# Attention of state tokens followed by two feed-forward nets: the opening's order, the third batch's route and the half chunk's place in the second sweep

## The chip, the cores and the metric

The kernel runs on one core of a Trainium2 chip. The metric is the device time of one launch in microseconds (us), the median over repeated runs. TensorE is called PE in the profile, its weight loads PEld, VectorE is DVE, ScalarE is ACT, GpSimd is POOL, and SP is the engine that issues nearly all DMAs. All matrix work is in 32-bit floats; most of it is done in three passes over a high and a low part (HIxHI, LOxHI, HIxLO), each part in the type fp32r.

## The reference, cut to what matters

```python
# x (8, 8, 512, 64): 8 batches, 8 heads, 512 tokens; state (8, 8, 32, 64): 32 state tokens
scores = scale * x @ state^T ; a = softmax(scores, over the 32 state tokens)
xread = a @ state                                   # (512 tokens)
scores2 = scale * state @ x^T ; a2 = softmax(scores2, over the 512 tokens)
sread = a2 @ x                                      # (32 state tokens)
x = concat([xread, sread], axis=tokens)             # 544 tokens a batch, 4352 in all
x = relu(x @ w_in)**2 @ w_out                       # 512 -> 2048 -> 512
a = x @ w1 ; b = x @ w2 ; out = ((a * b) @ w3) @ w_out2   # 512 -> 1024 -> 1024 -> 512
```

The weights come as 64-bit floats and are turned into 32-bit ones on the chip.

## The kernel before, in words

**Tokens.** The 512 tokens of batch b are chunk c = b (c = 0..7). The 8 x 32 state tokens make a ninth chunk, c = B = 8, of 256 columns: half a chunk.

**First stage (up to about 690 us).** The loop `order` runs over tiles (c, f): 16 tiles f of 128 hidden units for each chunk. The chunks 0 and 1 are interleaved (c0 f0-3, c1 f0-3, c0 f4-7, c1 f4-7, c0 f8-15, c1 f8-15), and then each chunk follows alone; "tile 20" below is the twentieth of this order, counted from 0. For each tile PE makes h (`h_tile`, L442: 6 matmuls), ACT and DVE make relu, square and the split (`act_h`), and two tiles later PE adds into four y banks (`y_tile`, L480: 12 matmuls). Between the tiles stand side jobs: `side[i]` behind h of tile i and `late[i]` behind the y part. They hold the conversions of weights from 64 bits (`conv`, five DVE instructions and one ACT instruction, and for w_out a split), `make_sw` (state times w_in, L413, 16 matmuls, needed by four h tiles), and the attention of the batch that comes next (`att_slots`).

**Attention of a batch** (`att_steps`): transposed x (`xpose` or `turn_x`), `scores` (L290), the softmax over x tokens (`soft2`, then `a2_T`, `sread`, `sread_T`) and that over state tokens (`soft1a`, `soft1b`, `a_T`). Batches below `BLK` = 3 take the PE route: x comes as rows (`load_x`), ACT copies it (`make_x`), PE transposes it with 16 matmuls against the identity (L277) and ACT copies the result; `soft1a` and `a_T` transpose on PE, too (L321, L345). Batches from `BLK` on take the block route: x is loaded twice, once as blocks of 32 columns (`load_xb`, eight DMAs of 64 KB for four heads) that DVE transposes block by block (`turn_x`, L257), once as rows (`load_xn`); `soft1a` and `a_T` transpose on DVE (L316, L341).

**The opening** (L513 to L542) loads the state of the first four chunks on ACT's queue (`load_st(0)`), x of batch 0, four half blocks of w_in, w_out's first block, x of batch 1 and the other half of the state; then batch 0's attention up to `at[1]`, whose last DVE instruction is `first`; the DVE work of `side[0]` is queued behind it.

**What sets the order.** A planner puts the instructions of each engine into one fixed order, from the program's order and its own estimate of when each is ready; `tc.issue_after(ins)` queues those instructions of a block that run on the same engine as `ins` behind it. Each engine then works in order. PSUM has eight banks: two "m" (side jobs), two "h", and "y0" to "y3". A tile tag with n buffers makes its n+1st user wait. The loads of weights, of `load_x` and of `load_xb` share the tag "raw" with three buffers. DMAs use eight semaphores in turn, so that a ninth waits until the first has landed; the queue behind it on the same engine waits with it.

**Second stage.** w3 times w_out2 is made first (`w34_rows`), so that the second net is a product (a*b) and one matmul. Its hidden units are done in two sweeps of half each (s = 0, 1). In each sweep pairs of chunks go through `quad` (L795, seven products) and `out_tile` (L876); `ab9` (L850) and `out_tile(B, ...)` do the same for the half chunk. `out_tile` of sweep 0 stores partial sums (`o_scr`), that of sweep 1 loads them (`load_o`), adds and writes the output, in one DMA of 256 KB for a chunk's tile and four of 64 KB for the half chunk's. Sweep 0 begins with the half chunk, sweep 1 ends with it. Between the sweeps `make_w` splits the weights of the second half and two DMAs load the second half of w34 (L950) into the buffers that sweep 0's last `out_tile` reads.

Of the kernel before, what the change touches and what calls it, by code (L numbers as in the profile page):

```python
# [8 lines left out]
F32 = mybir.dt.float32  # L9
# [11 lines left out]
def kernel(  # L21
# [24 lines left out]
    P = 128  # L46
# [9 lines left out]
    HI, LO = 0, 1  # L56
    BLK = 3

# [12 lines left out]
    def bank_m(name):  # L71
        return psum.tile([P, 512], F32, tag="m", bufs=2, name=name)
# [194 lines left out]
    def att_steps(b):  # L267
# [69 lines left out]
        def a_T(r):  # L337
            e = v["e1", r].rearrange("p k n -> p (k n)")
            if b >= BLK:
                ps = v["S", r]  # L340
                nc.vector.transpose(out=ps, in_=e)  # L341
            else:
                ps = bank_m("ps_a")
                for j in range(J):
                    nc.tensor.transpose(ps[:, j * P:(j + 1) * P], e[:, j * P:(j + 1) * P], ident)  # L345
            t = pa.tile([P, 2, 512], F32R, tag=f"aT{r}", bufs=2, name=f"aT{r}")
            aT_t[b, r] = t
            return split(t[:, HI], t[:, LO], ps)
# [40 lines left out]
    def att_slots(b):  # L389
        if b >= B:  # L390
            return [[] for _ in range(NF)]
        xp, sc, s2, s1a, s1b, at, a2t, sr, srt = att_steps(b)
        if b >= BLK:
            return [
                [sc], [], [s2[0], s1a[0]], [],
                [s1b[0], s2[1]], [a2t[0]], [at[0], s1a[1]], [sr[0]],
                [s1b[1], srt[0]], [a2t[1]], [at[1]], [sr[1]], [srt[1]], [], [], [],
            ]
        return [
            [xp[0]], [xp[1]], [xp[2]], [xp[3]],  # L400
            [sc], [s2[0]], [a2t[0]], [s1a[0], s2[1]],
            [sr[0], s1b[0]], [srt[0]], [a2t[1], at[0]], [sr[1], s1a[1]],
            [srt[1], s1b[1]], [at[1]], [], [],
        ]

    SW = {}

    def make_sw(b, fg, cols=slice(0, 512)):
        pss = [bank_m("ps_sw") for _ in range(G)]
        for k in range(HG):  # L410
# [84 lines left out]
    def load_st(half):  # L495
# [3 lines left out]
        for k in range(HG):  # L499
            for r in range(G):  # L500
                (nc.sync if half else nc.scalar).dma_start(
                    t[k * NS:(k + 1) * NS, :, r, :],
                    state[half * (B // 2):(half + 1) * (B // 2), 2 * k + r].rearrange("b n d -> n b d"),
                )
        st.append(t.rearrange("p b r d -> p b (r d)"))

    def make_st(half):
# [3 lines left out]
        nc.scalar.copy(stT[:, 4 * half:4 * half + 4].rearrange("p b k n -> p (b k n)"), ps)  # L511

    load_st(0)  # L513
    load_x(0, 0, True)
    load_x(0, 1, True)
    load_win0(0, 0, True)
    make_x(0, 0, nc.vector)
    make_x(0, 1, nc.scalar)
    load_win0(0, 1, True)
    load_win0(1, 0, True)  # L520
    load_win0(1, 1, True)
# [3 lines left out]
    load_st(1)  # L525
    for g in range(G):
        make_x(1, g, nc.scalar, True)
    make_st(0)
    xp, sc, s2, s1a, s1b, at, a2t, sr, srt = att_steps(0)
    xp1, sc1, s21, s1a1, s1b1, at1, a2t1, sr1, srt1 = att_steps(1)  # L530
    for step in xp:
        step()
    sc()
    make_win0(0, 0)
# [5 lines left out]
    s1b[1]()  # L540
    make_sw(0, 0, slice(0, 256))
    first = at[1]()  # L542

    convs = [("win", 1, k) for k in range(ND)] + [("wo", f) for f in range(4, 8)]
# [30 lines left out]
    late = {}  # L575
    side[0] = [lambda: make_win0(1, 0), s2[0], lambda: make_win0(1, 1), xp1[0], xp1[1], a2t[0]]
    side[1] = [lambda: make_sw(0, 0, slice(256, 512)), lambda: make_wout(0), xp1[2], xp1[3], sr[0], s2[1], sc1]
    side[2] = [conv, s1a1[0], srt[0], a2t[1], s1b1[0], sr[1], at1[0]]
    side[3] = [conv, s21[0], srt[1], s1a1[1], a2t1[0], conv, s1b1[1], sw(1, 0), at1[1]]
    side[4] = [conv, s21[1], sr1[0], lambda: make_st(1)]  # L580
# [9 lines left out]
    for b in range(2, B):  # L590
# [5 lines left out]
        for g in range(G):  # L596
            i = 9 + g if b == 2 else (b - 2) * NF + 12 + g
            if b < BLK:
# [318 lines left out]
    make_pair(raw)  # L917
    for m in range(QM):
        ab9(m)
    for t in range(n_out(B)):  # L920
        out_tile(B, t, 0)
    for s, todo in enumerate((pairs, pairs[::-1])):
        for i, (c0, c1) in enumerate(todo):
            for m in range(QM):
# [3 lines left out]
                if m == 1 and i + 1 == len(todo) and s == 0:  # L928
                    raw = load_w(1)
            if i + 1 == len(todo) and s == 1:  # L930
                raw = load9()
            outs = [(c, t) for c in (c0, c1) for t in range(n_out(c))]
# [3 lines left out]
            for n, (c, t) in enumerate(outs):  # L936
# [3 lines left out]
                with tc.issue_after(last.ins):  # L940
                    if n == 0 and i + 1 < len(todo):
                        make_pair(raw)
                    if n == 0 and i + 1 == len(todo) and s == 0:
                        make_w(raw)
                if n == 3 and i + 1 == len(todo) and s == 1:
                    make9(raw)
            if s == 0 and i + 1 == len(todo):
                for j in range(N1 // 4):
                    w34_t[N1 // 4 + j] = wpool.tile([P, 2, 2, DM], F32R, tag="wi0", bufs=2, name="w34b")
                    nc.sync.dma_start(f32(w34_t[N1 // 4 + j]), w34_s[j])  # L950
    for t in range(n_out(B)):
        load_o(B, t)
    for m in range(QM):
        ab9(m)
    for t in range(n_out(B)):
        out_tile(B, t, 1)

# [28 lines left out]
```

## Time and profile before

| | us |
|---|---|
| time, median of 3 runs (lowest, highest) | 1285.98 (1285.95, 1286.9) |
| the profiled execution's own time | 1288.85 |
| its span | 1287.0 |
| PE busy in the span | 1253.1 (97%) |
| DVE busy | 798.0 (62%) |
| ACT busy | 655.1 (51%) |

The profiled execution is 2.87 us above the median of the runs. "Busy" counts an engine's instructions from start to end as the profile has them; PE's ends are modelled, so that what one matmul costs is read from the distance between starts.

### The profile page before, as it was taken

Reading aid. Unit: us, or ns where it says so; the run is one execution under the profiler, and the core shown is the slowest. Engines: PE = TensorE matmul, PEld = TensorE weight load, DVE = VectorE, ACT = ScalarE, POOL = GpSimd, SP = SyncE. Lnnn points to the kernel's source line nnn. Section 1 sums busy time; section 2 is a strip of 40 time slices with the busy share of each in tenths; the row PEclk is TensorE's granted clock in tenths of the full one; section 3 lists DMA queues with packets and bytes.
Section 4 is the critical chain, followed back from the end, with each engine's and each line's share of the span. In section 5 each row is a group of like instructions: output and inputs, shape, how many; then the busy total and the mean of one; then the engine's idle time right before and its main releaser. Section 6 shows DMA issues by size and latency. Waiting matters only on the chain.

```text
span 1287.0 us, 16895 instructions
## 1 busy us (share of the span) xinstructions
PE 1253.1 (97%) x6392; PEld 986.7 (77%) x6392; DVE 798.0 (62%) x1444; ACT 655.1 (51%) x1174; POOL 23.3 (2%) x22
## 2 busy tenths in 40 slices
PE   4899999999999999999999999999999999999998
PEld 2566677677777777777789888888888888778877
DVE  4998965868577575753243763746465656666652
ACT  4776765657566565655555543535353442424231
POOL 0000000000000000000000000000510000000000
PEclk8899999999999999999999999999999999999999
DMA  6146525454453634510222531021530415050323
GB/s 212 43 151 202 179 80 118 105 123 144 95 163 76 162 114 113 151 49 34 73 91 66 174 108 46 37 95 61 172 116 29 154 59 178 27 188 26 106 66 99
DMA packets 122962, 137.94 MB, mean 107 GB/s; under 512 B 71425, under 2 KB 75009, under 8 KB 122369
## 3 DMA queue, kind: packets, MB, share of 16 engines
q1 hardware_dynamic: 121728, 136.61, 35.0%
q8 instruction: 50, 0.82, 0.3%
q10 hardware_dynamic: 1152, 0.26, 0.1%
q14 instruction: 32, 0.25, 0.1%
HBM read 93.32 MB, written 43.52 MB: 106 GB/s over the span
## 4 chain that ended last, share of the span: by engine, by line
PE 88%; DMA 4%; DVE 3%; ACT 3%; issue 1%; SPq 0%; ACTq 0%; DVEq 0%
PE y L480 26%; PE po L876 14%; PE qa L795 10%; PE qd L795 7%; PE qc L795 3%; PE ps_w L680 3%; PE qe L795 3%; PE ps_sw L413 2%; DMA yscr<-yo 2%; PE ab L850 2%; PE ps_r L362 1%; DMA x<-in_x_dram 1%; PE ps_s L290 1%; DVE sw L85 1%; PE ps_w L665 1%
## 5 line engine op out<-in xcount | busy, mean ns | idle before, releaser
L480 PE MATMUL y<-ghl,wo 128*128 128x512 f32 (+1 forms) x1728 | 406.6, 381 | 3.2 <-DVE yo L487 1.5
L480 PEld LDWEIGHTS y<-ghl,wo 128*128 128x128 f32 x1728 | 308.5, 188 | 93.9 <-ACT r L428 18.4
L85 DVE TENSOR_TENSOR ghl<-r,ghl 128x512 fp32r<-128x512 f32 (+1 forms) x144 | 94.9, 659 | 162.1 <-ACT ghl L84 161.2
L795 PE MATMUL qa<-yq,wq 128*128 128x512 f32 x576 | 146.3, 390 | 0.7 <-ACT s L803 0.7
L795 PEld LDWEIGHTS qa<-yq,wq 128*128 128x128 f32 x576 | 107.6, 188 | 24.8 <-ACT s L803 1.8
L803 ACT COPY s<-qa 128x512 f32<-128x512 f32 x96 | 56.1, 587 | 138.3 <-PE qa L795 127.4
L795 PE MATMUL qd<-yq,wq 128*128 128x512 f32 x384 | 98.3, 390 | 0.0
L876 PE MATMUL po<-w34b,c 128*128 128x512 f32 x408 | 95.8, 391 | 0.3 <-DVE o L885 0.3
L876 PE MATMUL po<-w,c 128*128 128x512 f32 x408 | 95.2, 390 | 0.0
L876 PEld LDWEIGHTS po<-w34b,c 128*128 128x128 f32 x408 | 75.7, 188 | 18.1 <-DVE c L85 1.0
L430 ACT ACTIVATE r<-r 128x512 f32<-128x512 f32 (+1 forms) x144 | 87.5, 608 | 3.2
L876 PEld LDWEIGHTS po<-w,c 128*128 128x128 f32 x408 | 75.6, 188 | 17.3 <-DVE c L85 0.8
L84 ACT CAST ghl<-r 128x512 fp32r<-128x512 f32 (+1 forms) x144 | 85.8, 596 | 3.8 <-PE y L480 0.5
L795 PEld LDWEIGHTS qd<-yq,wq 128*128 128x128 f32 x384 | 71.8, 188 | 15.7 <-ACT s L803 1.0
L129 ACT ACTIVATE ce<-ce,ebias 128x512 int32<-128x512 int32 x72 | 52.1, 725 | 48.5 <-DVE ce L128 48.4
L807 DVE TENSOR_TENSOR s<-qa,s 128x512 f32<-128x512 f32 x32 | 22.1, 691 | 75.2 <-ACT s L803 75.2
L84 ACT CAST c<-s 128x512 fp32r<-128x512 f32 x64 | 39.6, 621 | 37.1 <-DVE s L824 36.7
L84 ACT CAST yq<-yraw 128x512 fp32r<-128x512 f32 x70 | 42.6, 622 | 24.6 <-DVE yraw L770 15.5
L885 DVE TENSOR_TENSOR o<-po,opart 128x512 f32<-128x512 f32 x34 | 23.3, 688 | 45.4 <-PE po L876 34.5
L85 DVE TENSOR_TENSOR yq<-yraw,yq 128x512 fp32r<-128x512 f32 x70 | 46.6, 682 | 5.4 <-ACT yq L84 5.1
L795 PE MATMUL qc<-yq,wq 128*128 128x512 f32 x192 | 49.5, 390 | 0.0
L152 DVE SCALAR_TENSOR_TENSOR ce<-raw,ce 128x512 int32<-128x512 int32 x72 | 49.1, 683 | 0.3 <-ACT ce L129 0.3
(548 smaller groups left out, 1812.4 us busy)
## 6 DMA issues: line engine op xcount, KB each, us to landing
raw<-in_moe_w_dram SPq DMA_DIRECT2D x32, 512.0 KB, 4.6
yraw<-yscr SPq DMA_DIRECT2D x56, 256.0 KB, 5.3
raw<-in_moe_w_out_dram SPq DMA_DIRECT2D x24, 512.0 KB, 4.0
yscr<-yo SPq DMA_DIRECT2D x48, 256.0 KB, 3.0
oscr<-o SPq DMA_DIRECT2D x34, 256.0 KB, 2.2
opart<-oscr SPq DMA_DIRECT2D x34, 256.0 KB, 3.2
out_dram<-o SPq DMA_DIRECT2D x32, 256.0 KB, 3.0
raw<-in_moe_w_in_dram SPq DMA_DIRECT2D x12, 512.0 KB, 3.9
```

The costliest lines, as they stand in the source:

```text
L84: nc.scalar.copy(hi, src)
L85: return nc.vector.tensor_tensor(out=lo, in0=src, in1=f32(hi), op=ALU.subtract)
L129: nc.scalar.activation(e, e, ACTF.Relu, bias=ebias, scale=8.0)
L152: nc.vector.scalar_tensor_tensor(out=e, in0=hw, scalar=-(2**31), in1=e, op0=ALU.bitwise_and, op1=ALU.bitwise_or)
L413: nc.tensor.matmul(pss[r][k * NS:(k + 1) * NS, cols], stT[rows, b, k, :], win_t[fg][rows, k, cols], start=True, stop=True, tile_position=( ...
L430: nc.scalar.activation(r[:, :n], r[:, :n], ACTF.Square)
L480: nc.tensor.matmul(y_ps[c, d][:, :n], wo_t[f][:, wi, d * P:(d + 1) * P], t[:, gi, :n], start=(f == f0 and k == 0), stop=(f == f1 - 1 and k ...
L680: nc.tensor.matmul(ps, t[:, wi, (j % 4) * P:(j % 4 + 1) * P], wo2_t[j][:, vi, :], start=(j == 0 and k == 0), stop=(j == N1 - 1 and k == 2),)
L795: nc.tensor.matmul(ps, W[w, kt][:, wi, m * P:(m + 1) * P], Y[v, kt][:, vi, :], start=(first and kt == 0 and k == 0), stop=(last and kt == ...
L803: nc.scalar.copy(t, ps)
L850: nc.tensor.matmul(pss[i][:, :NT9], w[:, wi, m * P:(m + 1) * P], Y[B, d][:, vi, :NT9], start=(d == 0 and k == 0), stop=(d == ND - 1 and k ...
L876: nc.tensor.matmul(ps, v[:, vi, t * P:(t + 1) * P], w[:, wi, :], start=(m == 0 and k == 0), stop=(m == QM - 1 and k == 2),)
```

## The change

It has five parts. (1) The opening issues everything on SP: x of batch 0 first, then two DMAs of w_in, then the eight of the state; an activation at the very start has ACT's table loaded; both copies of x are made on DVE; `make_st(0)` comes behind the transposes of x; the copies of batch 1's x come behind `at[1]` in the program. (2) In batch 0 `make_sw`'s first half and `a_T` use y banks instead of m banks; some steps of batch 0's and 1's attention move one place back. (3) `BLK` becomes 2, so that batch 2 takes the block route; its loads stand at tiles 14 and 15, its `turn_x` at 16 and 17, `load_xn` at 20 and 21. (4) For all batches on the block route the scores stand two tiles later, the next step one. (5) The half chunk leads sweep 1 as it does sweep 0.

```diff
-    BLK = 3
+    BLK = 2
@@ a_T
-                ps = bank_m("ps_a")
+                ps = bank_m("ps_a") if b else bank_y(2 + r, "ps_a")
@@ att_slots, b >= BLK
-                [sc], [], [s2[0], s1a[0]], [],
-                [s1b[0], s2[1]], [a2t[0]], [at[0], s1a[1]], [sr[0]],
-                [s1b[1], srt[0]], [a2t[1]], [at[1]], [sr[1]], [srt[1]], [], [], [],
+                [], [], [sc], [s2[0], s1a[0]],
+                [], [s1b[0], s2[1]], [a2t[0]], [at[0], s1a[1]], [sr[0]],
+                [s1b[1], srt[0]], [a2t[1]], [at[1]], [sr[1]], [srt[1]], [], [],
@@ make_sw
-    def make_sw(b, fg, cols=slice(0, 512)):
-        pss = [bank_m("ps_sw") for _ in range(G)]
+    def make_sw(b, fg, cols=slice(0, 512), banks=None):
+        pss = [banks(r, "ps_sw") if banks else bank_m("ps_sw") for r in range(G)]
@@ load_st
-                (nc.sync if half else nc.scalar).dma_start(
+                nc.sync.dma_start(
@@ opening
+    warm = const.tile([P, 1], F32, name="warm")
+    nc.scalar.activation(warm, ebias, ACTF.Exp, scale=0.0)
+    for g in range(G):
+        load_x(0, g, True)
+    load_win0(0, 0, True)
     load_st(0)
-    load_x(0, 0, True)
-    load_x(0, 1, True)
-    load_win0(0, 0, True)
-    make_x(0, 0, nc.vector)
-    make_x(0, 1, nc.scalar)
     load_win0(0, 1, True)
+    for g in range(G):
+        make_x(0, g, nc.vector)
...
     load_st(1)
-    for g in range(G):
-        make_x(1, g, nc.scalar, True)
-    make_st(0)
...
     for step in xp:
         step()
+    make_st(0)
     sc()
...
-    make_sw(0, 0, slice(0, 256))
+    make_sw(0, 0, slice(0, 256), bank_y)
     first = at[1]()
+    with tc.issue_after(first.ins):
+        for g in range(G):
+            make_x(1, g, nc.scalar, True)
@@ side jobs
-    side[0] = [lambda: make_win0(1, 0), s2[0], lambda: make_win0(1, 1), xp1[0], xp1[1], a2t[0]]
-    side[1] = [lambda: make_sw(0, 0, slice(256, 512)), lambda: make_wout(0), xp1[2], xp1[3], sr[0], s2[1], sc1]
-    side[2] = [conv, s1a1[0], srt[0], a2t[1], s1b1[0], sr[1], at1[0]]
-    side[3] = [conv, s21[0], srt[1], s1a1[1], a2t1[0], conv, s1b1[1], sw(1, 0), at1[1]]
+    side[0] = [lambda: make_win0(1, 0), lambda: make_win0(1, 1), s2[0], xp1[0], xp1[1]]
+    side[1] = [lambda: make_sw(0, 0, slice(256, 512)), lambda: make_wout(0), xp1[2], xp1[3], a2t[0], s2[1], sc1]
+    side[2] = [conv, s1a1[0], sr[0], a2t[1], s1b1[0], srt[0], at1[0]]
+    side[3] = [conv, s21[0], sr[1], srt[1], s1a1[1], a2t1[0], conv, s1b1[1], sw(1, 0), at1[1]]
...
-            i = 9 + g if b == 2 else (b - 2) * NF + 12 + g
+            i = (b - 2) * NF + (18 if b == 2 else 12) + g
@@ second stage
-    for m in range(QM):
-        ab9(m)
-    for t in range(n_out(B)):
-        out_tile(B, t, 0)
     for s, todo in enumerate((pairs, pairs[::-1])):
+        if s == 1:
+            make9(raw9)
+            for t in range(n_out(B)):
+                load_o(B, t)
+        for m in range(QM):
+            ab9(m)
+        for t in range(n_out(B)):
+            out_tile(B, t, s)
...
-            if i + 1 == len(todo) and s == 1:
-                raw = load9()
...
                     if n == 0 and i + 1 == len(todo) and s == 0:
+                        raw9 = load9()
                         make_w(raw)
-                if n == 3 and i + 1 == len(todo) and s == 1:
-                    make9(raw)
...
-    for t in range(n_out(B)):
-        load_o(B, t)
-    for m in range(QM):
-        ab9(m)
-    for t in range(n_out(B)):
-        out_tile(B, t, 1)
```

## Rows read from the trace of the kernel before

**Rows 1.** Busy time of the engines by stretch (start:end in us, length, then each engine's busy us and instructions, the granted share of PE's clock, DMA's busy share, GB/s). The stretches: the opening; tiles 0 to 3; 4 to 15; 16 to 31; 32 to 47 (chunk 2); 48 to 63 (chunk 3).
```profile
0.00:26.90 26.90, 9.61 (x56) 5.73 (x56) 12.78 (x26) 11.67 (x17) 0.70 (x6) 0.91 0.83 252
26.90:64.80 37.90, 33.50 (x197) 22.11 (x198) 32.32 (x77) 25.97 (x50) 0.00 (x0) 0.84 0.13 41
64.80:126.80 62.00, 59.24 (x296) 40.78 (x296) 55.63 (x109) 43.74 (x76) 0.00 (x0) 1.00 0.57 175
126.80:208.90 82.10, 81.79 (x444) 60.55 (x443) 61.16 (x122) 54.36 (x96) 0.00 (x0) 1.00 0.44 119
208.90:288.10 79.20, 77.13 (x411) 57.18 (x410) 54.09 (x107) 46.34 (x80) 0.00 (x0) 1.00 0.48 122
288.10:364.10 76.00, 75.70 (x411) 56.87 (x410) 51.98 (x103) 46.05 (x80) 0.00 (x0) 1.00 0.46 124
```
**Rows 2.** Issues of loads in the opening, from the timeline (start and length of a run of issues; SPq and ACTq are the engines' issuing queues); the next to last from the chain of work that ended last; the last, of the state's loads, us from issue to landing.
```profile
0.74 7.43 ACTq L501 DMA_DIRECT2D st<-in_state_dram  x8
0.74 0.40 SPq L121 DMA_DIRECT2D raw<-in_moe_w_out_dram  x1
1.19 0.97 SPq L222 DMA_DIRECT2D x<-in_x_dram  x2
...
13.19 9.48 SPq L501 DMA_DIRECT2D st<-in_state_dram  x8
...
12.00 8.63 DMA x<-in_x_dram
...
DMA to landing us min/median/max: 2.1/5.5/9.4
```
**Rows 3.** The opening's work from the timeline (start, length, engine, line, operation; in brackets the idle time before it and what ended it).
```profile
6.90 0.69 DVE L235 COPY X<-x 128x1024 f32<-128x1024 f32 x1 [6.04 <-DMA x<-in_x_dram]
...
9.49 1.04 ACT L233 COPY X<-x 128x1024 f32<-128x1024 f32 x1
...
11.06 1.09 PE L510 MATMUL ps_st<-ident,st 128*128 128x128 f32 x4 [11.06 <-DMA raw<-in_moe_w_in_dram]
...
11.94 3.73 PE L277 MATMUL ps_x<-ident,X 128*128 128x128 f32 x16
...
15.60 1.83 PE L290 MATMUL ps_s<-xT,stT 64*32 64x512 f32 x16
...
20.04 1.28 DVE L325 TENSOR_TENSOR e<-ps_n,mx 128x512 f32<-128x512 f32 x2
20.66 1.04 ACT L233 COPY X<-x 128x1024 f32<-128x1024 f32 x1 [2.08 <-DMA x<-in_x_dram]
21.61 0.62 ACT L330 ACTIVATE e<-e 128x512 f32<-128x512 f32 x1
...
25.30 0.69 DVE L335 TENSOR_TENSOR e<-e,sm 128x512 f32<-128x512 f32 x1
...
28.64 1.11 PE L345 MATMUL ps_a<-ident,e 128*128 128x128 f32 x4
...
30.41 0.69 DVE L85 TENSOR_TENSOR aT<-ps_a,aT 128x512 fp32r<-128x512 f32 x1 [0.81 <-ACT aT L84]
```
**Rows 4.** Who PE waited for (us in total, times, longest us).
```profile
PE ps_a L353 <- ACT e L310: 3.4, 1, 3.4
...
PE ph__2265 L442 <- ACT sw L84: 1.2, 1, 1.2
...
PE ps_sw L413 <- ACT S L296: 0.7, 1, 0.7
```
**Rows 5.** Two more stretches by engine, with the columns of rows 1.
```profile
22.20:32.30 10.10, 7.49 (x34) 4.37 (x34) 6.95 (x16) 4.25 (x8) 0.00 (x0) 0.50 0.31 107
...
39.30:46.00 6.70, 6.03 (x35) 4.25 (x35) 5.02 (x12) 4.00 (x10) 0.00 (x0) 0.50 0.00 1
```
**Rows 6.** The third batch's transposes on PE in the timeline (the next row gives the distance between starts); DVE's block transposes (ns, min/median/max); the stretch in which batch 3's first eight block loads ran and one of bulk loads, with the columns of rows 1.
```profile
130.91 0.60 PE L277 MATMUL ps_x<-ident,X 128*128 128x128 f32 x4
131.27 1.64 PE L442 MATMUL ph__1327<-aT,sw 128*128 128x512 f32 x6
...
L257 DVE STREAM_TRANSPOSE xT<-xb x20: 668/703/711, 213.0 to 507.6; 128x512 f32<-128x512 f32 x20
...
202.10:208.60 6.50, 6.50 (x30) 5.40 (x29) 2.23 (x5) 3.70 (x6) 0.00 (x0) 1.00 0.51 83
12.00:20.00 8.00, 6.57 (x41) 3.84 (x39) 5.13 (x10) 4.51 (x8) 0.00 (x0) 1.00 1.04 324
```
**Rows 7.** Between the sweeps: the second issue of w34's second half in the timeline, and us from issue to landing of both. The half chunk's products at the end, from the timeline.
```profile
1024.47 0.32 SPq L950 DMA_DIRECT2D w34b<-w34s  x1
...
DMA to landing us min/median/max: 6.7/7.0/7.4
...
1265.31 11.68 PE L850 MATMUL ab<-y9q,wq 128*128 128x256 f32 x96
```
**Rows 8.** The end, from the timeline; and the output's DMAs (count, KB each, median us from issue to landing).
```profile
1280.49 4.45 SPq L894 DMA_DIRECT2D out_dram<-o  x8
1282.49 0.69 DVE L885 TENSOR_TENSOR o<-po,opart 128x512 f32<-128x512 f32 x1 [2.03 <-PE po L876]
...
out_dram<-o SPq DMA_DIRECT2D x32, 256.0 KB, 3.0
...
out_dram<-o SPq DMA_DIRECT2D x8, 64.0 KB, 1.7
```

## The prediction

> **What bounds the kernel now.** Read the page's shares first: PE is busy for 97% of the span, so that time can only come out of PE's stalls, its slow stretches and its own work. Then the busy time by stretch [rows 1]: the opening of 26.9 us holds 9.6 us of PE work; tiles 0 to 3 take 37.9 us where four tiles of a full batch (76.0 us for 16) take 19; tiles 4 to 15 take 62.0 us where twelve of a full batch take 57; tiles 16 to 31 take 82.1, chunk 2 takes 79.2, and a batch after that 76.0. From there to the end there is little to win but the tail. Beside PE stands DVE: 32.3 of 37.9 us, 55.6 of 62.0 and 61.2 of 82.1 [rows 1]. Up to about tile 22 DVE's weight conversions run nearly without a break, so what is moved in this part has two engines to satisfy: PE and DVE must both get earlier.
>
> **Part 1 and 2, the opening.** Before, one weight load goes out ahead of x [rows 2]. It is 512 KB, at 324 GB/s [rows 6] 1.6 us. x's first copy starts at 6.90, the second at 9.49 on ACT, whose queue was busy with issuing the state's loads until 8.17 [rows 2, 3]. With x in front and both copies on DVE I put them at 5.3 and 7.0. The 16 transposes took 3.73 us [rows 3] and can start at about 6, so that they end near 10 (the second half waits for the second copy); before, they came behind the state's transposes at 11.06.
>
> What is late next is the state. Its eight loads now stand on SP behind four bulk loads; the first four go out at once (some 0.45 us each, to about 4.5), the other four wait each for one of the bulk loads in front to land, as the later eight did at 13.19, which took 9.48 us to issue [rows 2]. I take 8.0 for the last issue, plus the shortest landing, 2.1 [rows 2], plus 0.3: 10.4. Transposes 1.09 [rows 3] and a copy of some 0.6 put the scores at 12.2 in place of 15.60 [rows 3]: 3.4 us earlier. Bounds: if the state is no later than x itself, the scores start at 10.4 and 5.2 us are won; the far end is a rival below.
>
> The Trainium skill speaks of this move, in "DMA: Bandwidth & Descriptors", section "Issuing engines are not separate DMA queues": loads from several engines end on the same 16 DMA engines, and a second issuer saves only the time to issue. By this rule the eight issues cost only their own 3.6 us, the last goes out near 5.3, the state is there before x is transposed, and the sum below would be 1.8 us larger, 13.0. The trace does not bear it out: the eight issues on SP took 9.48 us, for the waits between them [rows 2], so I stay with 8.0.
>
> From the scores to the end of `first` (30.41 + 0.69 = 31.1 [rows 3]) it was 15.5 us. In it ACT copied batch 1's x (20.66 to 21.70) ahead of the first exponential, whose input was ready when the first of the two L325 ended, about 20.7 [rows 3]: 0.9 us go when that copy stands behind. The second `a_T` started at 28.64 [rows 3] behind products that shared the two m banks; its input was done at 25.30 + 0.69 = 26.0 [rows 3], and with y banks it follows `make_sw` at once: 2.0 us go (0 to 2.6). So `first` comes 3.4 + 0.9 + 2.0 = 6.3 us earlier, and DVE's conversions queued behind it start as much earlier.
>
> In tiles 0 to 3 PE waited 3.4 us for `a2_T`'s input [rows 4]; `a2t[0]` now stands one place back, and DVE no longer does `s2[0]` ahead of the conversion that `make_sw` needs. But PE then waits for that conversion, and the DVE total stays. I count 0.2 of this 3.4 us on top and make the opening 6.5 us in all. There is more to be had: PE's clock was granted 0.50, that is 1.2 in place of 2.4 GHz, from 22 to 32 and from 39 to 46 us [rows 5], each time after PE had stood idle. If the second idle time shrinks enough, that second stretch stays at full speed, worth up to 3 us of PE; but DVE is the other bound there, so I leave it to the low end.
>
> **Part 3, batch 2 on the block route.** PE loses 32 transposes (16 of L277, 8 each of L321 and L345): four take 131.27 - 130.91 = 0.36 us [rows 6], so 8 x 0.36 = 2.9 us. ACT loses six copies, off the path. DVE gains eight block transposes of 0.70 us [rows 6], 5.6 us, four of them by tile 17. Tiles 4 to 15 lose the x loads at tiles 9 and 10 from the three raw buffers that weights need: 0.5 us won (0 to 1.5). In tiles 16 to 31 the new loads hold two of the three buffers from tile 14 to 17, while the conversions for tile 20's h run. PE was busy 81.8 of 82.1 us there and DVE 61.2 [rows 1], so half of DVE's 5.6 us and its waits for loads may show in the first eight tiles and little later. I charge 1.6 us: net 1.3 us won in tiles 16 to 31. Bounds: nothing charged, 2.9 us won; all of DVE's 5.6 plus one wait of about 2 for loads, 7.6 - 2.9 = 4.7 lost.
>
> Against this part speaks the Trainium skill, "DMA: Bandwidth & Descriptors", section "Specifications": pieces under 512 bytes miss the line rate. Block loads move rows of 32 floats. The trace agrees: with them the DMA engines were busy 0.51 for 83 GB/s, with bulk loads 1.04 for 324 [rows 6], twice the engine time for a byte. By the rule the weights' loads behind them come late, which is the second rival; its chance below is taken from those two rows.
>
> **Part 4, later scores.** In chunk 2 the scores of batch 3 stand right ahead of `make_sw` for tile 36; it waited 0.7 us for ACT to empty the m banks, and the tile's first matmul 1.2 us for ACT's cast [rows 4]. With the scores two tiles later `make_sw` goes first. Chunk 2 took 79.2 us, the next 76.0 [rows 1]: I take 2.6 of the 3.2 (1.9, the two waits, to 3.2). In later batches there is no such gap, and nothing is won.
>
> **Part 5, the half chunk.** Its products (11.68 us [rows 7]) and its output move from the end to between the sweeps; the sum of PE's work is the same. Between the sweeps two things could be late. w34's second half: the second DMA went out at 1024.47 and took at most 7.4 us [rows 7], landing by 1031.9. It writes a buffer that PE's last `out_tile` of sweep 0 reads, so that this one ends before that issue; I estimate 1.5 us, for another issue stands between. 11.7 us of products follow, and the first use comes near 1023.0 + 11.7 = 1034.7, with 2.8 us to spare. And the split of the half chunk's input, four DVE instructions behind `make_w`: I charge 0.3 us (0 to 2). At the end the four small DMAs, issued over some 1.7 us and landing 1.7 later, become one of 256 KB: from the last DVE add's end (1282.49 + 0.69 = 1283.2 [rows 8]) to the span's end was 3.8 us; with one issue and a median landing of 3.0 [rows 8] and the same 0.2 to close it is 3.2: 0.6 won (0 to 1.6, if it lands sooner with nothing beside it).
>
> **Sum.** 6.5 + 0.5 + 1.3 + 2.6 - 0.3 + 0.6 = 11.2 us. From the profiled execution's 1288.85 this gives 1277.65; it stands 2.87 us above the median of the runs, which I take off: 1274.8 us.
>
> **The rivals.**
> - *Batch 1's copies still go first.* `issue_after` binds only instructions of the engine of `first`, DVE; the copies run on ACT, and their place is the planner's. It had put one copy ahead of each exponential. For it: before, its order had each copy ready just ahead of an exponential. Against: the copies now come last in the program, and x of batch 1 goes out eight issues later. x took from 12.00 to 20.6 [rows 2]; with 1.6 us fewer bytes ahead the copy would run at 19.3 to 20.5 plus 1.04, and the exponential, due near 17.3, would start near 21: 3.5 us of the opening go. 1278.3 us.
> - *DVE and the raw buffers bind around tile 20.* The loss case of part 3, 4.7 lost where 1.3 were won, is 6.0 us worse; of that I take four fifths, 4.8: 1279.6 us. For it: DVE's share in tiles 4 to 15 [rows 1] and the half-rate loads [rows 6]. Against: PE was busy for all but 0.3 us of tiles 16 to 31 with DVE at three quarters [rows 1].
> - *The opening's gain is given back.* The tiles that DVE bounds end when the weights' loads and conversions allow; if these don't follow, 1.5 of the 6.5 us arrive at tile 16, 5.0 less: 1279.8 us. For it: DVE was busy 55.6 of 62.0 us in tiles 4 to 15 [rows 1]. Against: the conversions start with `first`, and move with it.
> - *Slower: the state lands behind all the bulk.* If the state's loads fall behind w_in, w_out and batch 1's x on the one queue, as the second eight did, the last lands at 13.19 + 9.48 + 2.1 = 24.8 [rows 2], the scores start at 26.5 in place of 15.6, 10.9 us late. The banks, the copy and the 0.2 still give 3.1, the other parts 11.2 - 6.5 = 4.7: 10.9 - 7.8 = 3.1 us slower, 1289.1 us. It turns slower from a state landing at 21.7 on. Against it: in the program only two bulk DMAs after x stand ahead of the state.
>
> **How the numbers follow.** Chances: forecast 0.52, first rival 0.17, second 0.15, third 0.09, fourth 0.07. The forecast's own range, from the bounds above (the opening 2 more or 2.5 less, the second clock stretch, parts 3 to 5), is 1270 to 1278.5. For 8 in 10 the range takes in the two middle rivals and leaves out half of the third and the slow one: 1270 to 1281.5. Within 0.2% is 1283.4 to 1288.6, about what a measurement of this kernel can tell from no change. Faster: 0.52 x 0.97 + 0.17 x 0.93 + 0.15 x 0.85 + 0.09 x 0.7 = 0.85. Same: 0.08, slower: 0.07, most of it the fourth case.
>
> **What would show it.** Right: first h matmul near 22 to 23 us instead of 26.9; scores near 12; no ACT copy of batch 1's x ahead of L330; chunk 2 at 76 to 77 us, with the L413 wait on L296 gone; tiles 16 to 31 near 81; no PE gap over 1 us at the sweep's change; the span ending some 3 us after the last add. Wrong: scores at 15 or later; `ps_sw` waiting on `win` for several us near tile 20; L876 waiting for the load of L950. A total above 1283 would mean that two of the gains failed together.

## The result, and the profile after

The changed kernel took 1297.86 us (median of 4, 1295.57 to 1302.03), the kernel before 1286.26 (4 runs) beside it: a ratio of 1.0091, 95% interval 1.0079 to 1.0103. It is slower by 0.9%; 1274.8 was forecast. The profiled execution took 1298.17 us, its span 1296.0.

Busy time by stretch of the changed kernel, with the columns and stretches of [rows 1]: the opening; tiles 0 to 3; 4 to 15; 16 to 31; chunk 2; chunk 3.

```profile
0.00:24.10 24.10, 12.61 (x74) 8.22 (x74) 13.22 (x28) 11.55 (x19) 0.70 (x6) 0.92 0.80 244
24.10:60.00 35.90, 30.55 (x178) 19.91 (x177) 31.46 (x73) 24.80 (x47) 0.00 (x0) 0.87 0.31 89
60.00:121.90 61.90, 60.40 (x298) 41.87 (x299) 56.48 (x111) 42.25 (x75) 0.00 (x0) 1.00 0.53 168
121.90:216.20 94.30, 86.07 (x411) 59.01 (x410) 66.08 (x129) 52.68 (x92) 0.00 (x0) 0.96 0.45 112
216.20:294.90 78.70, 78.41 (x412) 57.18 (x411) 53.99 (x107) 45.83 (x80) 0.00 (x0) 1.00 0.45 120
294.90:371.40 76.50, 76.50 (x411) 57.06 (x410) 51.99 (x103) 46.08 (x81) 0.00 (x0) 1.00 0.47 126
```

Read it against [rows 1] as a ledger. The opening and tiles 0 to 15 together end 4.9 us earlier (121.9 against 126.8). Tiles 16 to 31 take 94.3 us where they took 82.1: 12.2 lost, and this one stretch decides. Chunk 2 wins 0.5; chunk 3 loses 0.5, and the later chunks up to the end of the first stage 1.7, nearly all of it in chunk 5. From the half chunk's first product to the end it is 519.9 us in both. In sum the span is 9.0 longer.

In the lost stretch 33 instructions of PE are gone (411 for 444), yet its busy time rose from 81.79 to 86.07. The granted clock fell to a mean of 0.96; and PE's ends are modelled, so that part of a wait may be counted as busy (how much, no row shows). Some of who waited for whom there (us in total, times, longest):

```profile
DVE nm L301 <- ACT S L296: 6.7, 1, 6.7
...
PE ps_sw L413 <- DVE win L155: 2.7, 2, 2.1
...
PE y L480 <- ACT yo L489: 2.0, 1, 2.0
```

PE waits for a converted weight. DVE, which makes these, itself stood 6.7 us at batch 2's softmax (L301), whose scores were late. Why both were late shows in SP's issues in the timeline (start and length of a run of issues):

```profile
122.52 0.33 SPq L121 DMA_DIRECT2D raw<-in_moe_w_in_dram  x1
126.20 4.92 SPq L247 DMA_DIRECT2D xb<-in_x_dram  x8
131.22 0.43 SPq L121 DMA_DIRECT2D raw<-in_moe_w_in_dram  x1
132.03 5.04 SPq L247 DMA_DIRECT2D xb<-in_x_dram  x8
137.17 3.09 SPq L121 DMA_DIRECT2D raw<-in_moe_w_out_dram  x2
140.35 0.86 SPq L490 DMA_DIRECT2D yscr<-yo  x2
144.89 0.33 SPq L121 DMA_DIRECT2D raw<-in_moe_w_out_dram  x1
```

Batch 2's sixteen pieces occupy SP for 4.9 and 5.0 us; weights and stores of y stand between and behind them. From 118 to 150 us five weight loads went out and five conversions were made, where the kernel before had seven and eight. First the changed kernel, then the one before (in that window, by line: count, ns min/median/max, first and last start):

```profile
L149 DVE SCALAR_TENSOR_TENSOR cm<-raw,cm x5: 683/686/692, 120.4 to 137.0; 128x512 f32<-128x512 uint32 x5
L121 SPq DMA_DIRECT2D raw<-in_moe_w_out_dram x3: 333/347/433, 137.2 to 144.9; - x3
L121 SPq DMA_DIRECT2D raw<-in_moe_w_in_dram x2: 333/382/432, 122.5 to 131.2; - x2
```

```profile
L149 DVE SCALAR_TENSOR_TENSOR cm<-raw,cm x8: 678/680/685, 122.1 to 149.5; 128x512 f32<-128x512 uint32 x8
L121 SPq DMA_DIRECT2D raw<-in_moe_w_out_dram x4: 328/330/373, 134.0 to 144.9; - x4
L121 SPq DMA_DIRECT2D raw<-in_moe_w_in_dram x3: 333/333/333, 122.8 to 130.9; - x3
```

The opening in the timeline (in brackets the idle time before, and what ended it), to set beside [rows 2, 3]:

```profile
2.78 5.33 SPq L501 DMA_DIRECT2D st<-in_state_dram  x8
...
8.35 0.72 ACT L129 ACTIVATE ce<-ce,ebias 128x512 int32<-128x512 int32 x1 [6.12 <-DVE ce L128]
...
9.60 1.97 PE L277 MATMUL ps_x<-ident,X 128*128 128x128 f32 x8 [1.99 <-ACT xT L282]
...
13.18 1.96 PE L290 MATMUL ps_s<-xT,stT 64*32 64x512 f32 x16 [0.68 <-ACT stT L511]
...
18.86 1.23 ACT L330 ACTIVATE e<-e 128x512 f32<-128x512 f32 x2 [0.23 <-DVE e L325]
19.99 1.98 ACT L233 COPY X<-x 128x1024 f32<-128x1024 f32 x2
...
24.95 0.69 DVE L85 TENSOR_TENSOR aT<-ps_a,aT 128x512 fp32r<-128x512 f32 x1 [0.20 <-ACT aT L84]
```

The scores came 2.4 us earlier (13.18 for 15.60), ACT's copies of batch 1's x now stand behind both exponentials, and `first` (the last row) ended at 25.6 in place of 31.1.

### The profile page after: what moved, and what is told of

Read it like the earlier page. It is cut to its first block, busy times and chain, and to the rows that moved or that the text cites. A ratio compares the mean times of both kernels' runs of the same rounds, so it can differ in the third digit from the quotient of the medians.

```text
span 1296.0 us, 16876 instructions
## 1 busy us (share of the span) xinstructions
PE 1260.9 (97%) x6360; PEld 986.8 (76%) x6360; DVE 805.1 (62%) x1453; ACT 651.6 (50%) x1168; POOL 23.1 (2%) x22
## 4 chain that ended last, share of the span: by engine, by line
PE 87%; DVE 6%; DMA 3%; ACT 2%; issue 1%; SPq 0%; DVEq 0%; ACTq 0%
PE y L480 25%; PE po L879 13%; PE qa L798 10%; PE qd L798 6%; PE ps_w L683 3%; PE qc L798 3%; PE qe L798 3%; PE ps_sw L413 3%; PE ab L853 2%; DMA yscr<-yo 1%; PE ps_r L362 1%; PE ps_s L290 1%; DMA out_dram<-o 1%; DVE yq L85 1%; PE ps_a L353 1%
## 5 line engine op out<-in xcount | busy, mean ns | idle before, releaser
L129 ACT ACTIVATE ce<-ce,ebias 128x512 int32<-128x512 int32 x72 | 52.0, 722 | 42.5 <-DVE ce L128 42.5
L413 PE MATMUL ps_sw<-win,stT 64*32 64x512 f32 (+1 forms) x528 | 46.2, 594 | 8.2 <-DVE win L155 6.4
```

The lines of the kernel that those rows point to most:

```text
L129: nc.scalar.activation(e, e, ACTF.Relu, bias=ebias, scale=8.0)
L413: nc.tensor.matmul(pss[r][k * NS:(k + 1) * NS, cols], stT[rows, b, k, :], win_t[fg][rows, k, cols], start=True, stop=True, tile_position=( ...
```

## The experiments

All ran in the manner of the result above; "before" is the kernel before on the same chip in the same job (medians 1286.7 to 1287.2). Stretches are of the profiled execution.

**Which part costs.** e1 is the change with batch 2 back on the PE route; e2 to e4 put one part or two into the kernel before.

```diff
# e1 (in the changed kernel); e2 is the reverse, with part 4, in the kernel before
-    BLK = 2
+    BLK = 3
-            i = (b - 2) * NF + (18 if b == 2 else 12) + g
+            i = 9 + g if b == 2 else (b - 2) * NF + 12 + g
```

e3 moves the half chunk to the head of sweep 1; e4 has the opening alone (parts 1 and 2).

> The changed kernel with batch 2 back on the PE route (BLK = 3, its x loads at tiles 9 and 10). Theory A (batch 2's block route, with its loads and block transposes among the conversions of tiles 14 to 22, costs the time): the 13 us lost in tiles 20 to 31 go, the 5 us won before tile 16 stay: 1279 to 1283 us, tiles 20 to 31 in 60 us. Theory B (the earlier opening puts the planner's whole order off): no better than 1294 us. Theory C (the later scores): no better than 1294 us.

> The kernel before with BLK = 2, the new places of batch 2's loads and the later scores, nothing else. Theory A: 13 us slower in tiles 20 to 31, some 1297 to 1301 us. Theory B: within 3 us of the kernel before, 1283 to 1289 us.

> The kernel before with the half chunk in front of the second sweep, nothing else. Forecast of the prediction: 0.3 us won. The two profiles show both kernels' last parts equally long (from the first half chunk's product to the end), so theories A, B and C all expect 1285.5 to 1287 us.

> The kernel before with the new opening alone (one queue, x in front, y banks, steps of batches 0 and 1 moved back). Theory A: the opening's gain as the changed profile has it at tile 16, 4.9 us, arrives at the end: 1280 to 1283 us. Theory B: no gain or a loss, 1286 us or more. A third view (the tiles to 20 are bound by the conversions' loads, and the gain is given back there): 1285 to 1287 us.

| | median us (lowest to highest, runs) | ratio to before, 95% | tiles 16 to 31, us |
|---|---|---|---|
| e1_after_pe_route | 1287.16 (1283.27 to 1290.58, 10) | 0.9999 [0.9986, 1.0013] | 85.8 |
| e2_before_block_route | 1299.03 (1294.64 to 1302.12, 4) | 1.0090 [1.0063, 1.0116] | 91.2 |
| e3_before_half_first | 1286.38 (1284.52 to 1287.24, 10) | 0.9993 [0.9984, 1.0002] | 82.2 |
| e4_before_opening | 1290.79 (1282.32 to 1293.42, 10) | 1.0020 [1.0005, 1.0036] | 85.5 |

Part 3 (with part 4) makes the whole slowdown by itself (e2), as theory A has it; e2's profiled execution (1294.64 us) was its fastest, so that its stretch shows less of the loss than its median. Without it the change is level with before (e1), where A expected 1279 to 1283; and the opening alone gives nothing, as theory B has it, though at tile 4 it was 5.6 us ahead. So there are two causes, and they were followed apart.

**Part 3: what about it costs.** e5 gives the pieces of batch 2 two buffers of their own; e6 moves loads and turns four tiles ahead; e7 moves the scores and all behind them to slots two tiles later.

```diff
# e5
-        t = raw_tile(False, f"xb{b}_{g}")
+        t = raw_tile(b == 2, f"xb{b}_{g}")
# e6
-            i = (b - 2) * NF + (18 if b == 2 else 12) + g
+            i = (b - 2) * NF + (14 if b == 2 else 12) + g
# e7
-            late[(b - 1) * NF + i] = steps
+            late[(b - 1) * NF + (i + 2 * (b == 2)) % NF] = steps
```

> After, with the two block loads of batch 2 in buffers of their own (the ring of 16 that later holds w_out) in place of two of the three raw buffers; places, sizes and SP's order are unchanged. Stretch looked at: tiles 20 to 32, 60.5 us before, 73.8 after. Theory R (the conversions lose raw buffers to x, so their loads come late and DVE with them): the stretch falls to 64 to 67 us and the time to 1289 to 1292. Theory O (the loads and turns are late for their slot; DVE, ACT and TensorE each stand in order behind the scores of batch 2): x lands hardly earlier, the stretch stays at 71 to 74 us, DVE's idle 6.7 us at L301 stays at 5 or more, the time 1295 to 1299. Theory W (the added work on DVE and TensorE doesn't fit there): the same as O here.

> After, with batch 2's block loads four tiles earlier (tiles 10 and 11), its turns at 12 and 13 and its plain loads at 16 and 17; the scores keep their slot at tile 18. Theory O (late x holds the scores and all that stands behind them in order): the scores find their operands, DVE's wait at L301 falls below 2 us, tiles 20 to 32 take 65 to 68 us, the time is 1289 to 1292. Theory R (raw buffers): the shortage only moves four tiles ahead, tiles 8 to 32 together stay within 2 us of after's, the time 1296 to 1300. Theory W (work doesn't fit): as R.

> After, with the whole chain of batch 2 (scores, both softmaxes, transposes, squaring) two tiles later; loads and turns keep their places. Theory O: by tile 20 both halves of x are turned, DVE's wait at L301 falls below 2 us, tiles 20 to 32 take 65 to 69 us, the time is 1289 to 1293. Theory R: raw buffers and conversions are as late as in after; the stretch 72 to 75 us, the time 1296 to 1300. Theory W: as R, or worse, since the work then has fewer tiles: up to 1302.

All three failed as cures of the time: 1304.04 us (1.0131 [1.0116, 1.0146]), 1297.71 (1.0086 [1.0067, 1.0104]) and 1300.95 (1.0107 [1.0091, 1.0124]). Tiles 16 to 31 took 93.0, 91.9 and 90.6 us. e7 tells nothing on theory O: the planner left the copy of the scores (L296) at 151.26 us, where the changed kernel had it at 150.94; and its chunk 2 took 84.3 us for 78.7. e5 tells the most. With buffers to spare its 16 pieces still stood on SP in front of the weights:

```profile
123.99 1.15 SPq L247 DMA_DIRECT2D xb<-in_x_dram  x2
127.93 0.35 SPq L121 DMA_DIRECT2D raw<-in_moe_w_in_dram  x1
128.32 4.17 SPq L247 DMA_DIRECT2D xb<-in_x_dram  x6
132.59 0.43 SPq L121 DMA_DIRECT2D raw<-in_moe_w_in_dram  x1
133.07 7.03 SPq L247 DMA_DIRECT2D xb<-in_x_dram  x8
140.20 0.91 SPq L121 DMA_DIRECT2D raw<-in_moe_w_out_dram  x2
```

Eight issues took 7.03 us, and the next weight went out at 140.20. (That e5 is 6 us slower than the changed kernel is another matter: tiles 4 to 7, below.) In e6 the pieces took the raw buffers instead: between 113.98 and 124.01 no weight load went out at all. Yet from tile 8 to tile 31 e6 took 129.0 us for 133.8; it lost 5.0 in tiles 4 to 7, as e5 did, so that its time may hide a part of a cure. So the pieces now go to GpSimd's queue: in buffers of their own (e9), the same four tiles earlier (e10), and in the shared raw buffers (e13).

```diff
-                    nc.sync.dma_start(
+                    (nc.gpsimd if b == 2 else nc.sync).dma_start(
                         t[p0:p0 + NS, k * 512:(k + 1) * 512]...
```

> After, with batch 2's sixteen block pieces in buffers of their own (as in e5_after_own_buffers) and issued by GpSimd's queue in place of SP's. In e5 SP issued its pieces from 124.0 to 139.6 and the conversions' next raw load stood behind them until 140.2. Theory Q (that queue is what holds the conversions): raw loads go out every 3 to 5 us as before, the waits for win k 3 and for the scores shrink with them, tiles 20 to 32 take 63 to 67 us (after 73.8, e5 72.5), the time is 1286 to 1291. Theory O (the late scores of batch 2 and what stands behind them in order, whatever the loads do): 70 us or more, 1295 or more. Theory E (the small pieces slow the DMA engines themselves): raw loads land 5 us and more after issue, the stretch 68 to 72.

> As e9_after_own_queue, with loads and turns four tiles earlier (tiles 10 to 13), so that x waits for the scores. If Q is the whole cause: as e9 within 2 us. If the scores' lateness still costs by itself in e9 (theory O's part): 2 to 6 us less than e9 in tiles 20 to 32, DVE's wait at L301 under 2 us, the time 1284 to 1288. If E: tiles 8 to 32 together no better than in e9.

> After with batch 2's block pieces issued by GpSimd's queue, in the shared raw buffers. With e5 (buffers alone, tiles 20 to 32 72.5 us) and e9 (both, 64.8) this makes the square. If SP's queue is the whole cause: 63 to 67 us there, the time as e9, 1288 to 1294. If both are needed (the raw loads lack a buffer as long as x holds two of three): 69 to 74 us, the time 1294 to 1299.

| | median us | ratio to before, 95% | tiles 4 to 7 | tiles 16 to 31 | tiles 20 to 31 | DVE's wait at L301 |
|---|---|---|---|---|---|---|
| changed kernel | 1297.86 | 1.0091 [1.0079, 1.0103] | 22.4 | 94.3 | 73.8 | 6.7 |
| e5, buffers | 1304.04 | 1.0131 [1.0116, 1.0146] | 27.3 | 93.0 | 72.5 | 5.5 |
| e13, queue | 1297.54 | 1.0083 [1.0067, 1.0098] | 27.2 | 88.2 | 64.2 | 1.3 |
| e9, both | 1291.66 | 1.0044 [1.0026, 1.0062] | 27.2 | 85.5 | 64.8 | 2.5 |
| e10, both and early | 1290.42 | 1.0029 [1.0016, 1.0042] | 24.3 | 81.6 | 60.4 | none |

The square is plain in the stretch: buffers alone give 1.3 us, the queue alone 6.1, both 8.8, with the turns earlier 12.7, and the stretch is again where it was before (82.1). In e13 the loss moves forward: tiles 16 to 19 took 24.0 us where the changed kernel took 20.5, because the pieces still held raw buffers (e9, with its own, took 20.7). Its two stretches (tiles 16 to 19, and 20 to 31), and e10's tiles 16 to 31, with the columns of [rows 1]:

```profile
126.60:150.60 24.00, 22.65 (x98) 13.87 (x97) 19.91 (x37) 12.33 (x21) 10.55 (x16) 1.00 0.61 157
150.60:214.80 64.20, 61.94 (x316) 43.16 (x314) 46.38 (x93) 40.34 (x71) 0.00 (x0) 1.00 0.39 106
```

```profile
122.80:204.40 81.60, 81.37 (x411) 57.08 (x410) 65.11 (x129) 53.98 (x94) 0.00 (x0) 1.00 0.44 122
```

By the expectations: e9's stretch came as Q has it, its time 0.7 us above the range. e10's stretch is 4.4 us below e9's, which is not Q as the whole cause but the other case: the late scores of batch 2 cost by themselves. Its time is 2.4 above that case's range, for waits of copies of y at 76, 98 and 451 us (next part). e13 has the stretch of one case and the time of the other. Its time doesn't follow its stretch because tiles 4 to 7 took 4.8 us longer than in the changed kernel, with PE waiting 1.6 us for a copy of y; e5, e6 and e9 lost as much there. In these and in e10 the first store of y at 68 to 71 us landed after 5.1 to 5.4 us, in the changed kernel, e1, e4 and e7 after 3.1 to 3.2. None of the edits touches that store, and why it landed later is open; so the square is read from the stretch alone, one execution each. One reservation: with buffers and queue of their own, e9's and e10's pieces went out at 22 to 36 us, so these two take away every contact with the weights' loads at once, that on the DMA engines included. In e13 the pieces went out at 131 to 142 us, among the weights' loads.

**The opening: where its lead went.** In e4's trace the lead was lost between tiles 24 and 28 (from 3.4 us ahead to 0.3 behind). Who waited from 168 to 184 us, and after it, for the window 174 to 186, how long the stores of y took to land:

```profile
DVE yo L487 <- DMA yscr<-yo: 4.3, 1, 4.3
ACT yo L489 <- DMA yscr<-yo: 2.5, 1, 2.5
PE y L480 <- DVE yo L487: 2.3, 1, 2.3
```

```profile
DMA to landing us min/median/max: 2.3/2.8/4.5
```

Tag "yo" has two buffers, so the third copy waits for the first store. One store landed 4.5 us after issue; PE waited 2.3 us, and its granted clock then was 0.50 for 3.4 us. e8 and e11 add a third buffer for the first four batches, to the opening and to the kernel before; e12 to the change without part 3, e14 to the whole change. Room for it comes from the conversions' mask buffers (tag "cm", one in place of two), in the control e11 as well.

```diff
-                o = pa.tile([P, 512], F32, tag="yo", bufs=2, name="yo")
+                if c < 4 and len(yo_n) % 3 == 2:
+                    o = att.tile([P, 512], F32, tag="yo3", bufs=1, name="yo")
+                else:
+                    o = pa.tile([P, 512], F32, tag="yo", bufs=2, name="yo")
+                yo_n.append(o)
-        m = att.tile([P, 512], I32, tag="cm", bufs=2, name="cm")
+        m = att.tile([P, 512], I32, tag="cm", bufs=1, name="cm")
```

> Before with the change's opening alone (parts 1 and 2, as in e4_before_opening: 1290.79), and for the first four batches a third buffer for the copies of y that wait to be stored, taken from the attention pool (its place comes from the mask buffers of the conversions, one in place of two, all of whose users are on DVE in order). Theory Y (the 3 to 5 us that the opening gains are lost where the third copy of y waits for the store two before it, which an instruction fetch had delayed): the gap of 2.3 us at tile 25 goes, the lead at tile 40 stays at 2 us or more, the time is 1282 to 1286. Rival S (conversions and sw set the time by tile 28 whatever the opening gives): the gap is shifted elsewhere, the lead at tile 40 is again under 0.5 us, the time 1288 to 1291.

> Control for e8_opening_third_yo: before with the third buffer for copies of y alone. Theory Y (the buffer only keeps what the opening gains): before has only a wait of 1.3 us of this kind, at 100.8 us, so 1284.5 to 1287. Rival (the buffer itself is the gain, and the opening gives nothing): 1282 to 1284, as e8.

> After with batch 2 back on the PE route (as e1_after_pe_route, 1287.16) and the third buffer for copies of y: the change without part 3. By Y it keeps the opening's gain: e8's 1283.2 less 0.3 to 0.8 for the half chunk first and at most 2.5 for the later scores: 1280 to 1283.5. If it stays at 1286 or more, later scores or half first cost what e8 gains.

> After with the third buffer for copies of y alone. If part 3's stall is apart from the wait of y's copies: the gaps at 155 and 196 us go, part 3's waits stay, tiles 20 to 32 take 70 to 73 us, the time is 1292 to 1296. If y's copies were the larger part of the stall: under 66 us and under 1288.

| | median us (runs) | ratio to before, 95% |
|---|---|---|
| e8, opening | 1283.19 (10) | 0.9967 [0.9957, 0.9978] |
| e11, before | 1288.07 (10) | 1.0011 [1.0002, 1.0021] |
| e12, change without part 3 | 1282.87 (5) | 0.9964 [0.9951, 0.9977] |
| e14, whole change | 1295.73 (4) | 1.0067 [1.0052, 1.0081] |

The buffer alone gives nothing (e11, 1 us above the forecast for it); with the opening it turns +0.2% into -0.33%. The gap at tile 25 is gone in e8, and the lead at tile 40 is 3.4 us. In the whole change it gives some 2 us, and tiles 16 to 31 still take 93.4: the two causes are apart.

**Does the block route then pay?** e15 has all three (own buffers and queue, early, third buffer). e16 and e17 widen the third buffer to seven batches (`c < B - 1`) in the block route and the PE route.

> After with batch 2's block pieces in their own buffers, on GpSimd's queue and four tiles earlier (as e10, 1290.42), and the third buffer for copies of y. If the block turns give back TensorE's time once nothing disturbs the loads: e12's 1282.87 less up to 2.5, so 1280 to 1283. If they cost something else that e10 hid: 1284 to 1288.

> As e15_after_all_three (block pieces of batch 2 in own buffers, on GpSimd's queue, four tiles earlier), with the third buffer for copies of y in the first seven batches. If the wait at 451 us was what set e15 back: it goes, and the time is 1283.5 to 1286, level with or above e17. If the block turns give TensorE's time back: below e17 by 1 us or more.

> As e12_pe_route_third_yo (the change without part 3), with the third buffer for copies of y in the first seven batches: e12 had no wait of 0.6 us or more of this kind after tile 16, so the same as e12, 1281.5 to 1284.

e15: 1287.93 us (1.0008 [0.9999, 1.0017]), within the range of its second case. Against e14, which has the third buffer alone, that is 7.8 us by medians: the loss of part 3 is cured in the time, too. But e15 was level with e12 at tile 80 (435.6 and 435.3 us), waited 2.5 us for a copy of y in batch 4, which had no third buffer, and lost 3.1 more behind tile 128. e16: 1283.03 (8 runs, 0.9968 [0.9957, 0.9978]); e17: 1280.31 (5 runs, 1278.56 to 1281.48; 0.9949 [0.9936, 0.9961]), faster than the kernel before and the changed one. Tiles 16 to 31 of e16, then of e17:

```profile
120.00:203.40 83.40, 81.96 (x411) 56.97 (x410) 66.34 (x132) 53.98 (x94) 0.00 (x0) 1.00 0.43 120
```

```profile
123.00:205.50 82.50, 81.81 (x444) 60.40 (x443) 62.44 (x123) 54.88 (x97) 0.00 (x0) 1.00 0.42 119
```

Both came in below their ranges, by 0.5 and 1.2 us, and in the order that stands for no gain. In these tiles the block route saves 33 instructions of PE and no time; DVE does 3.9 us more. Tiles 16 to 23 alone, for the kernel before, e16 and e17, give a reason, though no run varied it:

```profile
126.80:168.30 41.50, 41.39 (x216) 29.80 (x215) 39.62 (x78) 31.43 (x56) 0.00 (x0) 1.00 0.56 161
```

```profile
120.00:161.80 41.80, 40.36 (x189) 26.24 (x188) 39.68 (x80) 28.98 (x51) 0.00 (x0) 1.00 0.48 151
```

```profile
123.00:165.50 42.50, 41.81 (x218) 29.67 (x216) 40.97 (x82) 32.66 (x59) 0.00 (x0) 1.00 0.50 159
```

DVE was busy for 95 to 96% of them in all three. In e16 PE waited there 0.5 us for a converted weight and 0.7 for the cast behind it: as I read it, PE has less work there and still goes at the pace of DVE's conversions.

The two times don't settle the route, though. At tile 128 e16 was still 1.6 us ahead of e17 (654.0 and 655.6 us; 3.0 at tile 16), and it lost 3.0 behind that, in the second stage, whose code is the same in both. Who PE waited for there for more than 0.4 us, in e16 and in e17:

```profile
PE qa L803 <- ACT s L811: 1.9, 2, 1.5
PE qd L803 <- ACT s L811: 0.5, 1, 0.5
```

```profile
PE qa L803 <- ACT s L811: 0.5, 1, 0.5
```

Why ACT's copy came later in e16 was not tried.

## Why the prediction was wrong, step by step

**Parts 1 and 2, the opening (6.5 us): the size nearly right, its arrival wrong.** The state's last issue was at 2.78 + 5.33 = 8.1, against 8.0 in the text. The scores came 1.0 later than forecast, since the two halves of the transposes were 2.0 us apart, waiting for ACT to empty the banks; ACT's order had a step of a weight's conversion (L129) ahead of that copy, and this step waited for DVE until 8.35. The sum has no term for this. The exponential and the `a_T` steps went as written: `first` was 5.5 us earlier for 6.3. Tile 16 was 4.9 us earlier, tile 20 6.0. The first rival (copies first) and the slow one (state behind the bulk) are refuted by the same rows. What failed is the unwritten step after it, that a lead at tile 4 is a lead at the end. The third rival had a part of this with another mechanism; it blamed the conversions, and the copies of y were it. With a third buffer 4.0 us by medians arrive (e8).

**Part 3 (1.3 us won): the step that failed.** I charged 1.6 us for turns and loads together, and even the far bound, one wait of 2 us for loads, was too small: tiles 16 to 31 lost 12.2 us, 13.5 off the forecast. I priced the buffers, and the rate of small pieces on the DMA engines; e5 and e13 show that the buffers alone are the smaller term (1.3 us), and the larger one is in the order of SP's queue (6.1): weights behind 16 issues of some 0.5 us and the waits between them. The prediction had used that very effect for the state's loads (9.48 us for eight issues, [rows 2]) and not applied it here. The second rival named the right place at well under half the price (4.7 us lost at the worst). With queue and buffers cured, the lateness of batch 2's scores is left: 3.9 us, e10 against e9.

On such queues the Trainium skill's "DMA: Bandwidth & Descriptors", section "Issuing engines are not separate DMA queues", says that a second issuing engine saves only the time to issue, which is usually small. The runs agree that the time to issue is what can be saved: sixteen pieces took SP 9.96 us, and another queue won 6.1 us in tiles 16 to 31 (e13). They don't agree that it is small, where what is queued behind is what the bottleneck waits for.

The credit of 2.9 us for PE's transposes failed too. They did go (411 instructions for 444), but e16 and e17 take 83.4 and 82.5 us: [rows 1]'s "PE busy 81.8 of 82.1" was read as PE bound by its own work, and DVE's 61.2 of 82.1 as slack of a quarter. But that is an average: DVE was busy 39.62 of the first 41.5 us and 21.53 of the other 40.6, so that in tiles 16 to 23 there are two bounds. The credit of 0.5 us for tiles 4 to 15 came, and more (61.9 us in e16, 63.1 in e17).

**Part 4 (2.6 us): mostly not there.** Chunk 2 took 78.7 us for 79.2. The `make_sw` wait of [rows 4] went, as written, and tiles 32 to 35 fell from 20.8 to 16.1 us, but 36 to 39 grew from 21.1 to 24.1 and 40 to 47 from 37.3 to 38.5: the work and its waits moved back within the chunk. Beside e4 and e8 (80.3 and 80.4, old slots, new opening) e1 and e17 (78.4 and 78.9) show 1.4 to 2.0, but e4's and e8's granted clock was at a mean of 0.98 there. At full clock the old slots took 79.2, 79.3 and 78.8 us (before, e3, e11), the new ones 78.4, 78.6 and 78.9 (e1, e2, e12): at most 0.9. Part 4 alone wasn't run.

**Part 5 (0.3 us): right.** e3 gives 0.9993 [0.9984, 1.0002]. w34's second half went out at 1031.05 and 1033.40, and PE went from the half chunk's products to `out_tile` without a stop (products from 1032.13 for 11.68 us, next at 1043.65). The end is shorter, as priced (last add ends at 1293.17, span at 1296.0: 2.8 us, 3.2 forecast):

```profile
1285.05 8.49 SPq L892 DMA_DIRECT2D out_dram<-o  x4
...
1292.48 0.69 DVE L888 TENSOR_TENSOR o<-po,opart 128x512 f32<-128x512 f32 x1 [2.03 <-PE po L879]
```

**Off the profile.** I took 2.87 us off for before's profiled execution standing above its median; the changed kernel's stands 0.3 above, so 2.6 us of the miss are not in the stages at all. What the profiled execution of before had more than its other runs isn't known.

Open: some kernels wait for copies of y at about 450 to 460 us (1.7 us in the changed kernel, 2.6 in e10, 2.5 in e15) and e12 doesn't; why it comes there was not tried.

## What to carry to other kernels

Before small loads are added to a queue that also carries what the bottleneck needs, count the issues times their length, with the waits between them, and ask what stands behind; a free queue, buffers of their own and an earlier start decided here whether such loads cost 12 us or nothing. A stage that is gained early has to be followed to the end: a double buffer that just sufficed can give it all back. And a busy share is read by stage, for each engine: taking work from PE gave nothing where DVE, three quarters busy on the average of the stage, was busy for 95% of its first half.

## What the runs showed of the hardware

A wait of 2 us can cost more than itself. In e5 PE waited 1.8 us for a copy of y in tiles 4 to 7; its granted clock then was 0.50 (1.2 in place of 2.4 GHz) from 77.4 to 84.2 us, and the stretch took 27.3 us, 4.9 more than in the changed kernel with the same work. It need not: e10 waited 2.0 us at the same place, its granted clock stayed at 1.00, and the stretch took 24.3. What decides isn't shown. First e5's, then the changed kernel's, then e10's:

```profile
60.10:87.40 27.30, 25.48 (x121) 15.88 (x122) 19.68 (x42) 15.41 (x29) 0.00 (x0) 0.87 0.39 131
```

```profile
60.00:82.40 22.40, 22.35 (x122) 14.57 (x123) 19.80 (x42) 15.58 (x29) 0.00 (x0) 1.00 0.50 159
```

```profile
58.80:83.10 24.30, 22.34 (x122) 14.33 (x122) 19.62 (x42) 15.44 (x29) 0.00 (x0) 1.00 0.45 145
```

The slow store in e4 (4.5 us for a median of 2.8) ran while the profile's list of DMA queues for 176 to 183 us shows one packet of another kind, an instruction load of 16 KB:

```profile
q1 hardware_dynamic: 513, 0.95, 36.3%
q8 instruction: 1, 0.02, 0.9%
```

0.9% of 16 engines over 7 us is 1.0 us of one engine. The pair is not a single event: e1, e8, e11, e12 and e17 each show a store of 4.3 to 4.5 us with one such load at the same place, and e1 loses its lead there as e4 does (3.0 us ahead at tile 24, 0.7 behind at tile 28). That the load delays the store is a reading; no run varied it, and it leaves open why e4's runs spread over 11 us (before: 3.6 in that job).
